# One planned schedule, another queue model: a causal-attention and FFN kernel on one core

## The chip, the core and the metric

The kernel runs on one core of a Trainium2 chip. The time is the device time of one execution in microseconds; before the change it is 1059.81 us, the median of three runs (1059.1 to 1061.09). TensorE (PE) multiplies matrices, VectorE (DVE) and ScalarE (ACT) work element by element and on rows, GpSimd (POOL) does the same for data in on-chip memory, and the queue of SyncE (SP) issues all DMAs. Each engine executes its instructions in the order in which they stand in the program; a semaphore holds an instruction, and all behind it on that engine, until its data is there.

## The reference

```python
q, k, v: (8, 8, 576, 64) float32        # batch, heads, positions, width of a head
scores = q @ k.T / sqrt(64), masked where block_i < block_j   # blocks of 64 positions
attn   = exp(scores - max); attn = attn / (sum + 1e-9)
x      = (attn @ v), heads side by side -> (4608, 512)
h      = x @ w_in                       # (512, 2048)
g      = h * clip(h + 3, 0, 6) / 6
out    = g @ w_out                      # (2048, 512)
```

## The kernel before

The attention of one batch element and two heads is a *slot*; there are 32, numbered n. A slot has three groups g of three blocks of 64 query rows. The FFN works on pieces of up to 384 rows of x, and each piece on 16 blocks f of 128 columns of w_in.

To keep the accuracy of float32, a float32 matrix is split into two float16 parts, high and low, and a product is the sum of three float16 products. Slots 0 to 3 and the first FFN piece, which run while the weights are still being split, are computed in float32 instead (functions with 32 in their name).

A slot n from 4 on goes like this: qk loads q and k, qks splits them, a DMA transpose makes qkT; TensorE makes the scores s; VectorE takes row maxima (st), ACT the exponentials p with their sums, and VectorE and ACT the normalised, split probabilities phl; DMA transposes make pT, one for g = 0 (phl_0), one for g = 1 (phl_1), three for g = 2 (phl_6 to phl_8); TensorE multiplies with vhl into pv: pv_0 for groups 0 and 1, pv_1 for group 2. VectorE and ACT write the result to x. pT01, which holds the transposed probabilities of groups 0 and 1, has one buffer. FFN: h = x, win; ACT and VectorE make r and g; o = g, wout, which is stored by way of osb.

In slots 0 to 3 TensorE transposes itself: scores sf, exponentials pf, transposes pt, result pf by pT. The sums are applied differently there (`pv_group32`, L940): the reciprocals of three row sums become three diagonal blocks rd (a 128x64 identity, each row times its reciprocal); TensorE multiplies rd with a block matrix of ones (pr), so that the reciprocals stand along the free dimension, and ACT copies it to rb. Three rd make one pr, and there are 12 of these groups.

**What sets the order.** No instruction is issued when the program's text reaches it. A `Recorder` takes all of them, finds their dependencies, and `schedule` (L260) plays them through a plan: for each engine a clock, for each instruction a cost from a formula (`cost`, L205), for each buffer a time at which it comes free. Whenever an engine is free in the plan it takes the ready instruction with the lowest key; the keys come from tables of due times (AT for slots, FT for FFN pieces, AS and RT for the float32 slots, and so on, L26 to L55). An instruction that two engines can do (`scaled`, L144) goes to the one that the plan sees finish it earlier. The instructions are emitted in the order of their planned starts. So a change of one cost can move the order on all engines.

A DMA in the plan before: it lands after a fixed time and a time by its size; loads and stores, but not transposes, wait in addition for those before them.

Of the kernel before, what the change touches and what calls it, by code (L numbers as in the profile page):

```python
# [14 lines left out]
ALU = mybir.AluOpType  # L15
# [7 lines left out]
WX = 10  # L23
WY = 27

U = 2.788  # L26
AS = (7.494, 11.408, 15.3, 22.633)
AL = 14.807
PV0 = 2.519
TA, TR, PR = 2.197, 5.661, 0.677  # L30
QR = 3.417
PVA, PVB = 0.93, 1.25
PHS = 18
WLP = 0
WHA = 0
EXA = 8
QTH = False
EVR = 3
EVP = 2
PRO = True  # L40
MEM = 0

NMIN = 64
QL = 0.849
VL = 0.2
W0, WD = 4.938, 2.891
S0, SD = 57.576, 4.59
M0, MD = 34.073, 5
RT = (25.619, 42.369, 59.881, 71.242)
RS, RL, VL1 = 2.796, 15.216, 24.0  # L50
VM0, VMX = 10.452, 0.3
AT = ((4, 86.25), (6, 128.63), (8, 159.32), (10, 199.92), (12, 240.31), (14, 287.79), (16, 335.13), (24, 565.96), (32, 826.62))
FT = ((0, 28), (1, 100), (2, 168.81), (3, 239.13), (4, 279.57), (5, 356.87), (7, 505.16), (10, 740.96), (13, 988.23))
QP = 0.55
VP = 0.5  # L55
BLK = 64
EXPONENT_BITS = 0x7F800000
# [3 lines left out]
class Op:  # L61

    __slots__ = ("ways", "key", "preds", "joint", "n", "start", "end", "tiles", "eng", "half")


class Engine:
# [9 lines left out]
        return call  # L78


ADV = {("tensor", "a"): 60.0}


class Recorder:
# [3 lines left out]

    NAMES = ("tensor", "vector", "scalar", "gpsimd", "sync")
    LAT = {"tensor": 55, "vector": 37, "scalar": 39, "gpsimd": 65, "sync": 65}  # L90
    TURN = 95
    BIAS = {"vector": 250.0, "gpsimd": 500.0}
    EDGE = 0.0
# [66 lines left out]
    def add(self, ways):  # L160
        eng, method, args, kw = ways[0]
        outs, ins = self.operands(args, kw)
        last = self.ops[-1] if self.ops else None
        if eng == "tensor" and self.joint is not None and last and last.joint == self.joint:
            op = last
            calls, occ, _, _ = op.ways[eng]
            more, took, _ = self.cost(eng, method, args, kw, outs, ins)
            op.ways[eng] = (calls + [(method, args, kw)], occ + more, occ + took, False)
        else:
            op = Op()  # L170
            op.joint, op.n, op.ways = None, len(self.ops), {}
            for e, m, a, k in ways:
                op.ways[e] = ([(m, a, k)], *self.cost(e, m, a, k, *self.operands(a, k)))
            op.key = self.key - self.adv.get((eng, self.cls), 0.0)
            op.preds, op.tiles, op.start = {}, [], None
            op.half = eng == "tensor" and outs[0].ap[0][1] <= 64 and method == "matmul"
            if eng == "tensor":
                op.joint = self.joint
            self.ops.append(op)
        for a, w in [(a, False) for a in ins] + [(a, True) for a in outs]:  # L180
            if self.on_chip(a):
                self.touch(op, a, w)

    def touch(self, op, a, w):
# [17 lines left out]
        keep.append((op, w, p0, p1, b0, b1))  # L202
        self.hist[t.name] = keep

    def cost(self, eng, method, args, kw, outs, ins):  # L205


        n = self.count(outs[0])
        if method == "dma_start":
            nb = mybir.dt.size(outs[0].dtype)  # L210
            for _, c in list(outs[0].ap):
                nb *= c
            if kw.get("transpose"):
                occ = max(1290, 172 * nb / 32768 - 150)
                return occ, occ + (1100 if nb <= 4 * 32768 else 2100), False
            if eng == "gpsimd":
                return 1300, 2900 + nb / 170, False
            return 600, 2000 + nb / 170, False
        if eng == "vector":
            if method == "tensor_reduce":  # L220
                n = self.count(ins[0])
            else:
                ptr = any(isinstance(a, bass.AP) and self.count(a) == 1 for a in args[2:] if n > 1)
                ptr = ptr or n == 1 and method == "tensor_scalar_mul" and isinstance(args[2], bass.AP)
            wide = [a for a in ins if self.count(a) > 1 and not self.psum(a)]
            port = len(wide) > 1
            if method in ("tensor_scalar", "tensor_copy") and n > 1:
                if not any(self.psum(a) for a in outs + ins):
                    if len(outs[0].ap) == 2 or outs[0].ap[1][1] % 2 == 0:
                        n = n / (4 if mybir.dt.size(outs[0].dtype) + mybir.dt.size(ins[0].dtype) == 4 else 2)  # L230
                        port = True
            occ = 68 + 1.042 * n
            if method != "tensor_reduce" and ptr:
                occ += 57
            return occ, occ + 80, port
        if eng == "scalar":
            occ = 94 + 0.8335 * n
            if isinstance(kw.get("scale"), bass.AP):
                occ += 95
            if isinstance(kw.get("bias"), bass.AP):  # L240
                occ += 58
            if "accum_out" in kw:
                occ += 93
            return occ, occ + 105, False
        if eng == "gpsimd":
            if method == "memset":
                return 20 + 1.0 * n, 50 + n, False
            occ = 75 + (2.0 if method == "tensor_tensor" else 1.1) * n
            return occ, occ + 30, True
        f32 = mybir.dt.size(ins[0].dtype) == 4  # L250
        occ = max(n / 2.37, 26) * (4 if f32 else 1) + 2
        if f32 and method == "matmul":
            occ = max(occ, 200)
        if method == "transpose":
            occ = max(occ / 2, 100)
        if outs[0].ap[0][1] <= 64 and method == "matmul":
            occ = occ / 2
        return occ, occ + 172, False

    def schedule(self):  # L260
# [17 lines left out]
        for tag in want:  # L278
            if need[tag].max() > bufs[tag]:
                i = int(need[tag].argmax())  # L280
# [20 lines left out]
        dma = 0.0  # L301
        half = False
# [21 lines left out]
        while done < N:  # L324
            e = min((x for x in self.NAMES if pend[x] or avail[x]), key=lambda x: now[x], default=None)
            if e is None:
                raise RuntimeError("no order")
            t = now[e]
            p, a = pend[e], avail[e]
            while p and p[0][0] <= t:  # L330
                r, k = heapq.heappop(p)
# [5 lines left out]
            if e != "tensor":  # L337
                i = 0
                while i < len(a):
# [4 lines left out]
                    r = room(ops[k], t, full)  # L344
                    if r is None:
                        ways = ops[k].ways
                        if len(ways) == 1:
                            r = t
                        else:

                            mine = t + ways[e][2] + self.BIAS.get(e, 0.0)
                            r = min(
                                max(now[q], ready[k][q]) + ways[q][2] + self.BIAS.get(q, 0.0)
                                for q in ways if q != e
                            )
                            r = t if r >= mine else max(t + 50.0, t + mine - r)
# [6 lines left out]
            else:  # L363
# [4 lines left out]
                for i, (key, k, rd) in enumerate(a):  # L368
# [3 lines left out]
                    r = room(ops[k], t, full)  # L372
                    if r is None:
                        first.setdefault(h, i)
                        if h:
                            got_half += 1
                            for x in ops[k].tiles:
                                if x not in got:
                                    rd = max(rd, min(free[self.meta[x][0]]))
# [3 lines left out]
                if first:  # L383
# [6 lines left out]
                    i = first[h]  # L390
# [14 lines left out]
            o = ops[pick]  # L405
            calls, occ, took, shared = o.ways[e]
# [6 lines left out]
            if shared:  # L413
                t = max(t, port["gpsimd" if e == "vector" else "vector"])
                port[e] = t + took - 60.0
            if e == "tensor" and o.half != half:
                half = o.half
# [2 lines left out]
            o.eng, o.start, o.end = e, t, t + took  # L420
            while head < N and ops[head].start is not None:
                head += 1
            if calls[0][0] == "dma_start" and not calls[0][2].get("transpose"):
                nb = (took - (2900.0 if e == "gpsimd" else 2000.0)) * 0.8
                dma = max(dma, o.end - nb - 400.0) + nb
                o.end = max(o.end, dma + 400.0)
            now[e] = t + occ
            self.busy[e] += occ
            for x in o.tiles:
# [5 lines left out]
            for s, flow in succ[pick]:  # L435
                rs = ready[s]
                for q in rs:
                    r = t if q == e and (e == "tensor" or not flow) else o.end + self.LAT[q]
                    rs[q] = max(rs[q], r)
                ndep[s] -= 1  # L440
                if not ndep[s]:
                    for q in rs:
                        heapq.heappush(pend[q], (rs[q], s))
# [12 lines left out]
def kernel(  # L456
# [13 lines left out]
    nc = Recorder(tc.nc)  # L470
# [92 lines left out]
    ident2 = wpool.tile([P, BLK], F32, tag="ident2", name="ident2")  # L563
# [376 lines left out]
    def pv_group32(n, g):  # L940
        t = pT.pop((n, g))

        r = sums.pop((n, g))
        nc.vector.tensor_scalar(r, r, 1e-9, 1.0, op0=ALU.add, op1=ALU.mult)
        nc.vector.reciprocal(r, r)
        rd = sm.tile([P, GB, BLK], F32, tag="rd", bufs=2, name=f"rd{n}_{g}")
        for i in range(GB):
            nc.gpsimd.tensor_scalar(rd[:, i], ident2, r[:, i:i + 1], 1.0, op0=ALU.mult, op1=ALU.mult)
        if g == 0 or PRO:
            o = 2 if g else len(n_ev) % 3  # L950
            pr = ps_o.tile([P, GT], F32, tag=f"o{o}", name=f"pr{n}_{g}")
# [11 lines left out]
        for j in range(nj):  # L963
            i0 = max(0, 2 * j - 3 * g)
            kp = BLK if 2 * j + 1 > 3 * g + 2 else P
            a = i0 * NU[g] + j
            us = slice(a, a + (GB - 1 - i0) * NU[g] + 1, NU[g])
            for h in range(2):
# [4 lines left out]
                    start=(j == 0),  # L973
# [390 lines left out]
    for n in range(NPAIR):  # L1364
        t = AS[n]
        at(t, qk_load32, n, lead=AL)
        at(t, v_load, n, lead=AL)
# [6 lines left out]
    for n in range(NPAIR):  # L1374
        t = RT[n]
# [9 lines left out]
    for n in range(NPAIR, NSLOT):  # L1385
        t, d = line(AT, n), line(AT, n + 1) - line(AT, n)
# [86 lines left out]
```

## Time and profile before

| | us |
|---|---|
| median of 3 runs | 1059.81 (1059.1 to 1061.09) |
| profiled execution, span from first to last instruction | 1063.1 |
| last ACT instruction of that execution (the last osb) begins | 1059.37 |
| TensorE busy | 995.4 |
| VectorE busy | 833.9 |
| ScalarE busy | 635.8 |
| GpSimd busy | 75.9 |
| mean granted clock of TensorE | 0.980 of full |

No time of the profiled execution other than its span is shown; the span is 3.3 us above the median of the runs.

How to read it: a row of instructions names the engine, the operation, the tile written, an arrow and the tiles read, with buffer numbers left out. A line of waits says which engine's instruction waited for which other, for how many us in total, how often, and the longest. Since all instructions are emitted by the recorder, nearly all of them carry the same line (L452), and one goes by the names of tiles.

### The profile page before, as it was taken

The page shows a single profiled execution, that of the slowest core. Times are in us where ns is not written, and L with a number is a line of the kernel's source. Part 1 is how long each engine was busy: PE and PEld are TensorE (multiplying, and loading weights), DVE is VectorE, ACT ScalarE, POOL GpSimd, SP SyncE. Part 2 cuts the span into 40 slices and gives each one's busy share as a digit, 9 for nine tenths or more (in the row PEclk, how much of TensorE's full clock was granted, in tenths as well). Part 3 has the DMA queues.
Part 4 walks back from the last instruction along what each step waited for, and adds up shares of the span by engine and source line. Part 5 has one row for each costly group of instructions (what it writes and reads, how often), then busy time and mean ns, then how long its engine had stood idle before and what let it go on. Part 6 is the DMA issues. An engine that isn't in the chain of part 4 may idle for free. (4 is left out here: it accounts for less than half of the span.)

```text
span 1063.1 us, 28968 instructions
## 1 busy us (share of the span) xinstructions
PE 995.4 (94%) x11588; PEld 726.0 (68%) x11588; DVE 833.9 (78%) x2308; ACT 635.8 (60%) x1548; POOL 75.9 (7%) x259
## 2 busy tenths in 40 slices
PE   6978967999999999999999999999999999999998
PEld 4645646776777867667766666777767777777776
DVE  4888999999999999899899889787898875332322
ACT  4668757666657676666776565566556563343332
POOL 3132220000000000000000000000000000000000
PEclk8998988999999999999999999999999999999999
DMA  6756546898889887888888779647656533000000
GB/s 157 189 166 180 141 111 140 140 185 156 152 159 171 153 152 143 147 164 149 156 143 181 133 116 167 118 77 143 117 90 128 92 80 57 1 31 2 31 1 31
DMA packets 414199, 128.90 MB, mean 121 GB/s; under 512 B 403184, under 2 KB 403440, under 8 KB 414064
## 3 DMA queue, kind: packets, MB, share of 16 engines
q1 hardware_dynamic: 414064, 127.05, 61.4%
q8 instruction: 91, 1.49, 0.6%
q14 instruction: 44, 0.36, 0.1%
HBM read 45.09 MB, written 9.44 MB: 51 GB/s over the span
## 5 line engine op out<-in xcount | busy, mean ns | idle before, releaser
L452 PE MATMUL h<-x,win 128*64 128x384 f16 (+2 forms) x4720 | 437.0, 321 | 1.8 <-DVE win L452 1.6
L452 PE MATMUL o<-wout,g 128*64 128x512 f16 (+3 forms) x3444 | 430.9, 381 | 2.2 <-DVE g L452 2.2
L452 PEld LDWEIGHTS <-win 128*64 128x64 f16 x4608 | 296.8, 110 | 69.9 <-issue 2.2
L452 PEld LDWEIGHTS <-g 128*64 128x64 f16 x3360 | 221.6, 110 | 105.9 <-issue 2.0
L452 ACT ACTIVATE r<-h,eg,sh 128x384 f32<-128x384 f32 (+1 forms) x240 | 137.1, 593 | 131.5 <-PE h L452 130.8
L452 ACT ACTIVATE p<-s,st,esc 128x64 f32<-128x64 f32 (+1 forms) x280 | 163.1, 587 | 73.6 <-DVE st L452 53.6
L452 DVE SCALAR_TENSOR_TENSOR r<-r,eg,h 128x384 f32<-128x384 f32 (+1 forms) x192 | 113.4, 592 | 116.1 <-ACT r L452 116.0
L452 DVE SCALAR_TENSOR_TENSOR phl<-p,st,phl 128x128 f16<-128x128 f32 (+4 forms) x252 | 135.3, 582 | 0.7 <-ACT phl L452 0.6
L452 ACT ACTIVATE g<-r 128x384 f16<-128x384 f32 (+1 forms) x165 | 84.5, 513 | 85.8 <-DVE r L452 84.9
L452 DVE SCALAR_TENSOR_TENSOR g<-r,g 128x384 f16<-128x384 f32 (+1 forms) x192 | 102.7, 535 | 29.9 <-ACT g L452 29.4
L452 DVE TENSOR_REDUCE st<-s 128x1 f32<-128x64 f32 (+1 forms) x280 | 120.0, 447 | 4.1 <-PE s L452 3.8
L452 PE MATMUL s<-qkT 128*64 128x64 f16 (+7 forms) x1120 | 99.0, 289 | 10.0 <-ACT p L452 6.4
L452 PEld LDWEIGHTS <-vhl 128*64 128x64 f16 x1680 | 72.3, 111 | 41.2 <-issue 25.3
L452 PE MATMUL pv<-pT,vhl 128*64 128x192 f16 (+2 forms) x1680 | 75.1, 235 | 24.8 <-DMA pT<-phl 20.8
L452 ACT ACTIVATE phl<-p,st 128x256 f16<-128x256 f32 (+4 forms) x135 | 70.4, 556 | 34.4 <-DVE st L452 18.7
L452 PEld LDWEIGHTS <-qkT 128*64 128x64 f16 x1120 | 60.0, 111 | 35.4 <-issue 13.0
L452 POOL MEMSET p<- 128x64 f32 x140 | 21.4, 154 | 521.4 <-DVE phl L452 492.5
L452 ACT ACTIVATION_READ_ACCUMULATOR p<-s,st,esc 128x1 f32 x280 | 55.1, 197 | 0.0
L452 DVE TENSOR_SCALAR phl<-p,st 128x512 f16<-128x512 f32 (+4 forms) x117 | 46.0, 424 | 1.8
L452 DVE SCALAR_TENSOR_TENSOR qks<-qk,rs_q,qks 128x576 f16<-128x576 f32 x56 | 44.7, 817 | 0.0
L452 ACT ACTIVATE x<-pv 128x192 f16<-128x192 f32 (+1 forms) x61 | 22.0, 360 | 33.4 <-PE pv L452 30.7
L452 DVE TENSOR_REDUCE qkmx<-qk 128x2 f32<-128x1152 f32 x28 | 37.6, 1344 | 1.6 <-DMA qk<-in_k_dram 1.6
(154 smaller groups left out, 819.4 us busy)
## 6 DMA issues: line engine op xcount, KB each, us to landing
out_dram<-osb SPq DMA_DIRECT2D x35, 256.0 KB, 2.5
vnat<-in_v_dram SPq DMA_DIRECT2D x64, 128.0 KB, 2.9
qk<-in_q_dram SPq DMA_DIRECT2D x28, 288.0 KB, 3.6
qk<-in_k_dram SPq DMA_DIRECT2D x28, 288.0 KB, 4.4
rawo<-in_moe_w_out_dram SPq DMA_DIRECT2D x15, 512.0 KB, 4.6
rawi<-in_moe_w_in_dram SPq DMA_DIRECT2D x14, 512.0 KB, 4.0
pT<-phl SPq DMA_TRANSPOSE x140, 3.4
vnat<-in_v_dram SPq DMA_DIRECT2D x32, 32.0 KB, 2.7
```

What stands on the lines that cost most here:

```text
L452: getattr(eng, method)(*args, **kw)
```

## The change

1. In the plan every DMA, transposes included, goes through one queue: it begins at the earliest `lead` after its issue and after the one before it has ended, takes its bytes by a rate, and has landed `tail` after that; three kinds (load, store, turn) with three sets of numbers. An instruction of TensorE that depends on a DMA is planned 1250 ns after that (`MARGIN`).
2. The cost formulas of a DMA transpose and of ACT's sums are changed.
3. rd may be made by ACT or VectorE, and no longer by GpSimd.
4. The tables of due times are refitted. `EVP` decides in which memory bank the transposes pt of slots 0 to 3 land.

```diff
-U = 2.788
+U = 2.847
...
-QL = 0.849
+QL = 1.341
...
-EVP = 2
+EVP = 4
...
-ADV = {("tensor", "a"): 60.0}
+ADV = {("tensor", "a"): 67.44}
...
+    MARGIN = {"tensor": 1250.0}
+    QUEUE = {"load": (4137.0, -1860.0, 256.0), "store": (4137.0, -1860.0, 580.0), "turn": (4074.0, -2300.0, 182.0)}
...
+            op.queue = self.queue(args, kw) if method == "dma_start" else None
...
+    def queue(self, args, kw):
+
+        nb = mybir.dt.size(args[0].dtype)
+        for _, c in list(args[0].ap):
+            nb *= c
+        kind = "turn" if kw.get("transpose") else "load" if self.on_chip(args[0]) else "store"
+        lead, tail, rate = self.QUEUE[kind]
+        return lead, tail, nb / rate
...
-                occ = max(1290, 172 * nb / 32768 - 150)
+                occ = max(1290, 189 * nb / 32768 - 200)
...
             if "accum_out" in kw:
                 occ += 93
+                return occ, occ + 195, False
...
-            if calls[0][0] == "dma_start" and not calls[0][2].get("transpose"):
-                nb = (took - (2900.0 if e == "gpsimd" else 2000.0)) * 0.8
-                dma = max(dma, o.end - nb - 400.0) + nb
-                o.end = max(o.end, dma + 400.0)
+            margin = {}
+            if o.queue:
+                lead, tail, work = o.queue
+                dma = max(t + lead, dma) + work
+                o.end = dma + tail
+                margin = self.MARGIN
...
-                    r = t if q == e and (e == "tensor" or not flow) else o.end + self.LAT[q]
+                    r = t if q == e and (e == "tensor" or not flow) else o.end + self.LAT[q] + margin.get(q, 0.0)
...
         for i in range(GB):
-            nc.gpsimd.tensor_scalar(rd[:, i], ident2, r[:, i:i + 1], 1.0, op0=ALU.mult, op1=ALU.mult)
+            nc.scaled(rd[:, i], ident2, r[:, i:i + 1], "AV")
```

The instructions of TensorE and SP are the same ones in another order. On the other engines some that can be done by two have changed place: VectorE has 2300 instead of 2310, ACT 1244 instead of 1198, GpSimd 228 instead of 264; the rd are 25 on ACT and 11 on VectorE, where 36 were on GpSimd.

What moves is seen in the order of the instructions. The SP queue in slot 21, before and after (pT21 is written from phl21; qkT22 belongs to the next slot, qk24 and vnat are loads for later slots):

```order
L452 DMA_TRANSPOSE pT21_0_1605<-phl21_0_1611 128x8x128
L452 DMA qk24_1736<-in_q_dram 128x9x64
L452 DMA qk24_1736<-in_k_dram 128x9x64
L452 DMA_TRANSPOSE qkT22_1627<-qks22_1621 128x27x128
L452 DMA vnat2_100<-in_v_dram 128x4x64 x2
L452 DMA vnat2_100<-in_v_dram 64x2x64
L452 DMA_TRANSPOSE pT21_0_1605<-phl21_1_1636 128x18x128
```

```order
L467 DMA_TRANSPOSE pT21_0_1606<-phl21_0_1612 128x8x128
L467 DMA qk24_1751<-in_q_dram 128x9x64
L467 DMA qk24_1751<-in_k_dram 128x9x64
L467 DMA_TRANSPOSE pT21_0_1606<-phl21_1_1627 128x18x128
L467 DMA_TRANSPOSE qkT22_1642<-qks22_1636 128x27x128
L467 DMA vnat2_100<-in_v_dram 128x4x64 x2
L467 DMA vnat2_100<-in_v_dram 64x2x64
```

The transpose of phl21_1, on which pv21_0 waits, has moved ahead of the transpose of qks22 and of the loads of v.

TensorE at the last score block of slot 3 (sf3_8_1 is the second half of its scores, pf3_8 their exponentials, pt3_8_0 the transposes of these):

```order
L452 MATMUL sf3_8_1_549<-qkf3_0_180,qkf3_2_182 128x256
L452 MATMUL pt3_8_0_570<-ident_89,pf3_8_550 128x128
L452 MATMUL mb_q5_608<-qkmx5_603,one_96 64x2 x2
L452 MATMUL pt3_8_0_570<-ident_89,pf3_8_550 128x128
L452 MATMUL pt3_6_0_552<-ident_89,pf3_6_511 128x128 x4
```

```order
L467 MATMUL sf3_8_1_549<-qkf3_0_180,qkf3_2_182 128x256
L467 MATMUL o0_1_312<-wout_86,g0_11_493 64x256 x2
L467 MATMUL pr3_1_516<-rd3_1_515,halves_95 128x192
L467 MATMUL o0_0_311<-wout_86,g0_11_493 128x512
L467 MATMUL h0_13_557<-x0_81,win_85 128x192
L467 MATMUL pt3_6_0_552<-ident_89,pf3_6_502 128x128 x3
L467 MATMUL mb_q4_525<-qkmx4_520,one_96 64x2 x2
L467 MATMUL pt3_6_0_552<-ident_89,pf3_6_502 128x128
L467 MATMUL h0_13_557<-x0_81,win_85 128x192 x2
```

The transpose pt3_8_0 stood straight behind its scores; now it follows after these rows and after h0_13, o0_0, o0_1, mb_w5, h1_0 and pt3_7.

The diagonals of slot 0, group 2: on GpSimd before, on ACT now.

```order
L452 TENSOR_SCALAR sgo1_1_201<-rawo1_1_200 128x512
L452 TENSOR_SCALAR rd0_2_334<-ident2_94,sums0_2_242 128x64 x3
L452 MEMSET pf2_6_447 128x64
L452 TENSOR_SCALAR wout_86<-wout_86,rsio_88 128x512
L452 TENSOR_SCALAR rd1_1_378<-ident2_94,sums1_1_308 128x64 x3
```

```order
L467 ACTIVATE abo1_0_293,wacc1_290<-wout_86 128x512
L467 ACTIVATE rd0_2_331<-ident2_94,sums0_2_238 128x64 x3
L467 ACTIVATE pT1_1_344<-pt1_3_0_345 128x256
L467 ACTIVATE exi2_0_222<-x1_82 128x512
L467 ACTIVATE win_85<-win_85,rsio_88 128x2x256
```

They stood among GpSimd's work on the weights; they now stand among ACT's, between the maxima of one weight block (abo) and the copy of transposes of slot 1.

More of the change, by code (lines that the diff above doesn't have):

```diff
@@ L24 @@
 WY = 27
-U = 2.788
[L27 to L32, printed above, removed]
+U = 2.847
+AS = (7.494, 11.408, 15.3, 22.979)
+AL = 20.256
+PV0 = 2.145
+TA, TR, PR = 2.432, 5.661, 0.677
+QR = 3.473
+PVA, PVB = 0.916, 1.038
 PHS = 18
@@ L43 @@
 NMIN = 64
-QL = 0.849
[L45 to L54, printed above, removed]
+QL = 1.341
+VL = 0.415
+W0, WD = 5.472, 2.891
+S0, SD = 57.672, 4.668
+M0, MD = 33.973, 5.111
+RT = (24.007, 40.757, 58.269, 69.63)
+RS, RL, VL1 = 2.796, 28.901, 29.883
+VM0, VMX = 12.417, 0.323
+AT = ((4, 86.25), (6, 128.63), (8, 159.32), (9, 178.32), (10, 199.92), (12, 240.31), (14, 287.79), (16, 335.13), (24, 565.96), (32, 826.62))
+FT = ((0, 28), (1, 100), (2, 168.81), (3, 239.13), (4, 279.57), (5, 362.65), (7, 510.94), (10, 757.38), (13, 994.01))
+QP = 0.221
 VP = 0.5
@@ L61 @@
 class Op:
-    __slots__ = ("ways", "key", "preds", "joint", "n", "start", "end", "tiles", "eng", "half")
+    __slots__ = ("ways", "key", "preds", "joint", "n", "start", "end", "tiles", "eng", "half", "queue")
 class Engine:
```

## The prediction

> **What bounds the kernel now.** I read the page's busy lines first, then the same by stage, then TensorE's waits, and last the rows around the longest waits.
>
> ```profile
> span 1063.1 us, 28968 instructions
> PE 995.4 (94%) x11588; PEld 726.0 (68%) x11588; DVE 833.9 (78%) x2308; ACT 635.8 (60%) x1548; POOL 75.9 (7%) x259
> PEclk8998988999999999999999999999999999999999
> ```
>
> TensorE is busy 995.4 of 1063.1 us, so 67.7 us of idle time is the most that any order of the same work can win back, plus what the lowered clock costs (the digits of 8 at the start). The multiset of TensorE's instructions is the same before and after, so its work is no term. The stages, as windows over the span (columns: window, its length, busy PE, PEld, DVE, ACT, POOL, granted clock, DMA share, GB/s):
>
> ```profile
> 0.00:40.00 40.00, 30.33 (x138) 19.11 (x139) 22.44 (x66) 22.16 (x79) 10.85 (x41) 0.91 0.68 169
> 40.00:100.00 60.00, 50.44 (x282) 33.51 (x282) 50.08 (x130) 43.45 (x111) 18.43 (x25) 0.89 0.60 174
> 100.00:180.00 80.00, 65.13 (x473) 41.50 (x473) 77.73 (x210) 57.76 (x143) 18.00 (x36) 0.91 0.60 140
> 180.00:330.00 150.00, 144.47 (x1899) 110.36 (x1896) 144.94 (x431) 96.73 (x239) 6.85 (x37) 1.00 0.87 153
> 330.00:630.00 300.00, 283.61 (x3853) 207.42 (x3851) 275.77 (x808) 204.27 (x509) 12.90 (x72) 0.99 0.83 152
> 630.00:893.60 263.60, 255.72 (x3166) 188.98 (x3162) 213.77 (x584) 153.66 (x364) 8.84 (x48) 1.00 0.61 111
> 893.60:1063.10 169.50, 165.68 (x1794) 125.11 (x1794) 49.16 (x85) 57.77 (x106) 0.00 (x0) 1.00 0.04 15
> ```
>
> TensorE's idle time is 34.1 us in the first 180 us, 5.5 to 330, 16.4 to 630, 7.9 to 893.6 and 3.8 after it. From 893.6 on there is only FFN work behind an idle rest of the chip; nothing can be won there. VectorE is the second limit: it idles 17.6, 9.9 and 2.3 us in the first three stages and 5.1 and 24.2 in the next two. So between 100 and 330 us a wait of TensorE taken away is worth little unless VectorE's queue gets shorter too. Who TensorE waits for (total us, times, longest), first over the span, then to 180 us, to 630 and to 1063:
>
> ```profile
> PE pv L452 <- DMA pT<-phl: 20.8, 20, 2.5
> ...
> PE pr L452 <- POOL rd L452: 8.3, 5, 2.9
> PE pt L452 <- ACT pf L452: 8.3, 6, 6.1
> PE s L452 <- ACT p L452: 3.3, 1, 3.3
> ...
> PE pv L452 <- DMA pT<-phl: 15.8, 13, 2.5
> ...
> PE pv L452 <- DMA pT<-phl: 5.0, 7, 1.4
> ```
>
> After 180 us it is one thing: the PV matmul stands at the head of TensorE's queue while the transposed probabilities are still in a DMA. The clock is a second cost of the same waits. The windows in which the trace grants half the clock:
>
> ```profile
> 20.97:27.80 6.83, 6.18 (x24) 3.70 (x24) 1.97 (x5) 2.76 (x9) 0.29 (x1) 0.50 0.94 290
> 61.93:65.35 3.42, 3.42 (x13) 2.34 (x12) 2.49 (x6) 2.88 (x9) 0.15 (x1) 0.50 0.13 13
> 79.00:89.24 10.24, 7.43 (x20) 5.06 (x21) 7.66 (x20) 7.19 (x18) 3.48 (x7) 0.50 0.37 107
> 140.44:147.27 6.83, 3.78 (x17) 3.08 (x18) 6.12 (x19) 3.54 (x11) 0.49 (x3) 0.50 0.24 77
> 167.75:174.57 6.82, 3.53 (x42) 3.09 (x43) 6.82 (x24) 5.62 (x13) 1.23 (x2) 0.50 0.71 143
> 437.40:440.81 3.41, 3.41 (x28) 1.82 (x24) 2.57 (x7) 1.52 (x6) 0.30 (x2) 0.50 0.69 130
> 587.59:591.00 3.41, 3.41 (x24) 1.52 (x22) 2.38 (x10) 0.33 (x1) 0.15 (x1) 0.50 0.90 166
> ```
>
> The first three stand at or behind waits for POOL's rd, the fourth at the 6.1 us wait for ACT, the fifth at the 3.3 us wait, the last two behind the longest two waits for pT. TensorE is busy 31.2 us in them; at half the clock at most half of that, 15.6 us, is lost.
>
> **The change part by part.** *Readers of DMAs planned 1250 ns later, all DMAs in one modelled queue.* It adds no instruction. The two longest pT waits in the timeline, the second with the queue that issued the transpose (columns: start, us, engine, line, instruction, idle time before it and its releaser):
>
> ```profile
> 436.91 0.96 PE L452 MATMUL pv<-pT,vhl 128*64 128x192 f16 x16 [2.03 <-DMA pT<-phl]
> ...
> 572.61 5.24 SPq L452 DMA_TRANSPOSE qkT<-qks  x1
> 577.90 0.61 DVE L452 SCALAR_TENSOR_TENSOR phl<-p,st,phl 128x384 f16<-128x384 f32 x1
> 577.96 1.75 SPq L452 DMA_DIRECT2D vnat<-in_v_dram  x3
> 579.88 8.19 SPq L452 DMA_TRANSPOSE pT<-phl  x2
> 583.41 0.84 PE L452 MATMUL o<-wout,g 128*64 128x512 f16 x6
> 586.77 0.85 PE L452 MATMUL pv<-pT,vhl 128*64 128x192 f16 x18 [2.52 <-DMA pT<-phl]
> ```
>
> Before the second, VectorE delivers phl at 578.5, but SP still issues the 27-block qkT transpose (5.24 us) and three loads of v, and starts on pT at 579.88. In the new order of SP this slot has phl21_1 ahead of both. Over the 28 slots, qkT is issued between the first and second transpose of the slot in 24 before and in 8 now. It isn't the whole cause: the slots that had no qkT in between wait too. The mean wait is 20.8/20 = 1.04 us, under the 1.25 us margin, and the longest would keep 2.52 - 1.25 = 1.27. Bounds: 20.8 us gained, or nothing, if VectorE and not the DMA is what is late. I take 60%, 12.5 us, since VectorE has 5.1 + 24.2 us of idle time left between 180 and 630. With no wait near 2 us the last two clock windows go as well: half of 3.41 + 3.41, 3.4 us (bounds 0 and 3.4). Together -15.9.
>
> The Trainium skill, "TensorE: Matmul & The Clock Gate", section on HAM oscillation, has the clock fall only where TensorE idles longer than about 3.4 us. Here windows stand behind waits of 2.0 and 2.5 us, so the trace does not agree on the length; by the page alone the 3.4 us would not be there to win, and this term would be -12.5.
>
> Cost of the margin: pv later by 1.25 us keeps pT01 (one buffer) and phl2 occupied that much longer. Behind pv stand only h and o of the FFN, for which VectorE and ACT have been ready; I price it at nothing. If that cover is gone, each of 28 slots pays up to 1.25 us, 35 us: the upper bound of the unknown.
>
> *rd off GpSimd.* 36 instructions go; 25 land on ACT, 11 on VectorE.
>
> ```profile
> 56.62 3.89 POOL L452 TENSOR_SCALAR rd<-ident,sums 128x64 f32<-128x64 f32 x3 [1.16 <-DVE sums L452]
> ...
> L452 POOL TENSOR_SCALAR rd<-ident,sums x36: 313/320/2799, 10.7 to 147.5; 128x64 f32<-128x64 f32 x36
> L452 POOL TENSOR_SCALAR wout<-wout,rsio 128x512 f16<-128x512 f32 x7 | 7.1, 1013 | 26.9 <-DVE rsio L452 13.8 <-DVE sums L452 11.5 <-DVE wm L452 1.6
> L452 POOL TENSOR_SCALAR sgo<-rawo 128x512 f32<-128x512 f32 x7 | 5.5, 783 | 7.3 <-DVE sums L452 4.2 <-DVE wout L452 1.7 <-ACT abi L452 1.5
> L452 ACT ACTIVATE phl<-p,st 128x128 f16<-128x128 f32 x35 | 12.7, 392 | 7.0 <-DVE st L452 4.2 <-DVE esc L452 2.4 <-issue 0.3
> L452 ACT ACTIVATE pT<-pt 128x128 f32<-128x128 f32 x12 | 3.3, 275 | 2.8 <-PE pt L452 2.8
> L452 DVE TENSOR_SCALAR phl<-p,st 128x128 f16<-128x128 f32 x21 | 5.7, 289 | 0.6
> L452 DVE TENSOR_SCALAR dg_w<-ident,dg_w 2x2 f32<-2x2 f32 x8 | 1.7, 210 | 0.0
> ```
>
> (In the second row: shortest, median and longest in ns; in the others after the bar busy us and mean ns.) Three rd, 313 ns each at best, took 3.89 us on POOL ahead of the 2.9 us wait. On ACT one costs between 275 and 392 ns, I take 0.33: 8.3 us in a stretch (40 to 180) where ACT idles 38.8; hidden, save that an exp queued behind three rd comes 1 us later: +2 by estimate (bounds 0 and 12 groups x 1 = 12). On VectorE between 210 and 289, 0.25: 2.8 us, two thirds of it where VectorE is full: +1.8. What goes is 8.3 us of waits and, in the three windows behind them, half of 6.18 + 3.42 + 7.43, 8.5 us: 16.8 at most, 0 at least. VectorE's idle time in these stages (17.6 + 9.9, the first much of it the start) caps it; I take -6.
>
> The Trainium skill, "SBUF — State Buffer", section "Who interferes with whom", has a GpSimd instruction that reads SBUF and a VectorE one with two SBUF inputs shut each other out for a whole instruction. The 3.89 us agree: VectorE ran such instructions beside it. By that rule VectorE gains too; that result is the first rival.
>
> *Refitted tables.* They reorder everything to 180 us. The 6.13 us wait ahead of pt3_8 came straight behind sf3_8_1 (order above): the exp and its row maximum had no time. Now some fifteen groups of matmuls stand between. But in that wait VectorE did not idle:
>
> ```profile
> 140.00:143.10 3.10, 0.00 (x0) 0.00 (x0) 3.10 (x8) 0.64 (x3) 0.00 (x0) 0.57 0.00 0
> ...
> DVE vmax L452 <- DMA vnat<-in_v_dram: 8.0, 5, 2.4
> ```
>
> So of 6.1 + 3.3 us and half of 3.78 + 3.53 us, 13.1 in all, I take VectorE's idle time in that stage, -2 (bounds 0 and 13.1). VectorE's own waits for loads of v (8.0 us between 180 and 630) shrink with the later v_max; this is in the 60% above. New waits that another order brings: +4, by estimate; bounds 0 and the 35 above.
>
> **Sum.** -15.9 + 2 + 1.8 - 6 - 2 + 4 = -16.1. The profiled execution has a span of 1063.1, which lies 3.3 us over the median of the runs, 1059.81; the step is the same for both: 1063.1 - 16.1 = 1047.0 in a profile, 1043.7 for the median. I say 1044.
>
> **The rivals.** *VectorE freed (larger gain).* If POOL's rd also held VectorE up, for the shortest rd, 36 x 0.313 = 11.3 us, VectorE's queue in 40 to 330 us shortens, and the terms for rd and the tables double or better: -16.1 - 8 - 6 = -30, 1030. For it speaks that rd stands in the stages where VectorE is full; against it that POOL keeps other instructions of 783 to 1013 ns each there.
>
> *VectorE is late anyway (small gain).* 144.94 of 150 us busy: TensorE's waits for pT are then VectorE's lateness in another dress, and move to s, h and o. Left are the gain after 630 us, where VectorE idles 49.8 (5.0), a clock window or two (3.4) and a little at the start: -5 to -7, 1054.
>
> *The margin doesn't do what it says.* It counts from planned times; if the plan runs over 1.25 us ahead of the chip, the pv come no later against their data. Then -6 - 2 + 3.8 and new waits of 4: about 1059.6, no change.
>
> *The waits collect (slower).* TensorE runs further ahead of VectorE, stalls at s, for banks that exp has not read, in fewer and longer waits; each over 2 us brings a window of 3.41 us at half clock, 1.7 us lost. The 16.4 + 5.5 us of idle time stay, and eight such windows (two now) add 6 x 1.7 = 10; with rd's exps 2 late and nothing won at the start but 6: 1059.8 + 10 + 2 - 6 = 1066. It decides from where VectorE idles under some 10 us between 180 and 630 (29.3 now). For it: fullness of VectorE; against: of 20 pT waits only two brought a window.
>
> **How the numbers follow.** The forecast (1036 to 1052) 0.50; larger gain (to 1024) 0.13; small gain (1052 to 1057.5) 0.15; no change 0.06; slower 0.16. About 0.2%, 2.1 us, is what a measurement of this kernel can tell from no change. Faster by more: 0.78; within it: 0.06; slower: 0.16. The range leaves out a tenth at either end: 1029 to 1063.
>
> **What would show it.** The forecast is right if waits of pv for pT fall under 9 us, none of them near 2; if pr waits for nothing over 1 us; if half-clock windows are four or fewer; and if TensorE's idle time to 180 us falls from 34.1 to about 26. The small gain shows as the same idle time between 180 and 330 under other names (s, h, o waiting for DVE or ACT). The slower case shows as new windows at 0.50 after 180 us. The forecast is wrong in size if VectorE's idle time between 40 and 330 us stays at 17.3.

## The result

The changed kernel takes 1027.58 us, the median of four runs (1027.22 to 1028.61); the kernel before takes 1060.45 (1059.1 to 1065.02) beside it. The ratio is 0.968, with an interval of 0.9643 to 0.9717: 33 us less, where the forecast was 16 and its range ended 1.4 us above the measured time. The profiled execution has a span of 1026.8 us and a mean granted clock of 0.988 (0.980 before).

The page of the changed kernel: its span, the busy times, and the granted clock in 40 slices.

```profile
span 1026.8 us, 28995 instructions
PE 989.4 (96%) x11588; PEld 723.3 (70%) x11588; DVE 826.4 (80%) x2298; ACT 650.9 (63%) x1594; POOL 62.1 (6%) x223
PEclk9999989999999999999999999999999999999999
```

TensorE's idle time is 1026.8 - 989.4 = 37.4 us; it was 67.7. So 30.3 of the 36.3 us between the two spans are idle time (the medians lie 32.9 us apart), and 6.0 are shorter work: TensorE is busy 21.4 us in windows at half the clock, where it was 31.2, and half of that difference is 4.9 us. The first five windows of the prediction's table, and two of those at half the clock:

```profile
0.00:40.00 40.00, 31.99 (x165) 20.69 (x166) 25.87 (x84) 24.93 (x88) 6.92 (x29) 1.00 0.70 183
40.00:100.00 60.00, 55.38 (x327) 34.74 (x325) 58.42 (x147) 55.39 (x149) 13.68 (x16) 1.00 0.69 200
100.00:180.00 80.00, 68.45 (x564) 46.07 (x566) 74.67 (x212) 56.60 (x147) 12.64 (x22) 0.87 0.57 122
180.00:330.00 150.00, 146.08 (x1945) 111.18 (x1942) 147.66 (x438) 105.20 (x257) 7.39 (x41) 0.99 0.96 165
330.00:630.00 300.00, 296.43 (x4003) 216.10 (x4001) 287.62 (x843) 212.77 (x524) 13.65 (x75) 1.00 0.87 156
...
100.44:107.27 6.83, 5.91 (x16) 3.12 (x15) 4.86 (x13) 4.62 (x14) 1.89 (x4) 0.50 0.53 155
...
243.80:247.21 3.41, 3.41 (x36) 2.71 (x34) 3.29 (x13) 2.86 (x6) 0.15 (x1) 0.50 1.07 229
```

TensorE idles 8.0, 4.6 and 11.6 us in the first three stages, 24.2 to 180 us (34.1 before), then 3.9 and 3.6 (5.5 and 16.4). VectorE's idle time fell too: 1.6 us in the second stage (9.9 before), 2.3 in the fourth (5.1), 12.4 in the fifth (24.2); in the third it rose, from 2.3 to 5.3. The half-clock windows that remain are five, 23.9 us in all (the first and the last are shown; seven and 41.0 before), and none stands behind a wait for pT.

A window holds other work in each kernel. So here is the same by place in the program: when TensorE ends the last score block of a slot, and how long it has idled until then (the trace, lined up with the order of the instructions).

| to the end of slot | end before, us | end after | idle before, us | idle after | gained in idle time |
|---|---|---|---|---|---|
| 4 | 167.4 | 151.5 | 30.8 | 20.7 | 10.1 |
| 8 | 262.5 | 250.2 | 37.9 | 27.5 | 10.4 |
| 11 | 330.3 | 317.8 | 39.6 | 28.1 | 11.5 |
| 23 | 629.6 | 604.3 | 56.0 | 31.7 | 24.3 |
| last instruction | | | 63.9 | 33.6 | 30.3 |

(The idle time after TensorE's last instruction, 3.8 us in both kernels, is not in this table.) A third is gained by slot 4, nothing much from there to slot 11, and two thirds later.

TensorE's waits, the five largest and those for rd (total us, times, longest):

```profile
PE h L467 <- DVE r L467: 5.1, 3, 3.5
PE qt L467 <- DMA qf<-in_q_dram: 3.0, 2, 2.9
PE o L467 <- DVE g L467: 2.8, 4, 1.3
PE pt L467 <- ACT pf L467: 2.8, 6, 1.1
PE s L467 <- ACT p L467: 2.1, 6, 0.6
...
PE pr L467 <- ACT rd L467: 1.6, 2, 0.8
...
PE pr L467 <- DVE rd L467: 0.7, 1, 0.7
```

The largest row of before, pv waiting for pT, 20.8 us, has no successor: no such wait is left anywhere. pr waits 2.3 us instead of 8.3, pt for pf 2.8 instead of 8.3. All waits together are 31.9 us instead of 61.4: kinds of wait that shrank did so by some 46 us, and kinds that are new or grew add some 17, the largest h for r with 5.1 (pr for rd is counted as one kind, whichever engine makes rd).

The new diagonals (in ns: shortest, median, longest; then the time of the first and last):

```profile
L467 ACT ACTIVATE rd<-ident,sums x25: 331/338/356, 12.2 to 130.5; 128x64 f32<-128x64 f32 x25
L467 DVE TENSOR_SCALAR rd<-ident,sums x11: 236/249/255, 19.5 to 113.5; 128x64 f32<-128x64 f32 x11
```

And the chain that ended last, by engine (before: PE 21%, DVE 0%):

```profile
PE 28%; DVE 7%; DMA 1%; ACT 1%; issue 1%; SPq 0%; ACTq 0%; DVEq 0%
```

These shares can't be compared as they stand, because the chain can be followed further back here: to 625 us, where it ended at 822 us before. From 790 us on VectorE has no share of it in the changed kernel; its 7% lie earlier, where the chain of before doesn't reach.

### The profile page after: what moved, and what is told of

Same layout as the page of the kernel before. It is cut to its first block, busy times and chain, and to the rows that moved or that the text cites. A ratio compares the mean times of both kernels' runs of the same rounds, so it can differ in the third digit from the quotient of the medians.

```text
span 1026.8 us, 28995 instructions
## 1 busy us (share of the span) xinstructions
PE 989.4 (96%) x11588; PEld 723.3 (70%) x11588; DVE 826.4 (80%) x2298; ACT 650.9 (63%) x1594; POOL 62.1 (6%) x223
## 5 line engine op out<-in xcount | busy, mean ns | idle before, releaser
L467 ACT ACTIVATE g<-r 128x384 f16<-128x384 f32 (+1 forms) x161 | 82.1, 510 | 86.5 <-DVE r L467 85.1
L467 DVE SCALAR_TENSOR_TENSOR phl<-p,st,phl 128x256 f16<-128x256 f32 (+4 forms) x252 | 135.6, 582 | 0.6 <-ACT phl L467 0.2
L467 ACT ACTIVATE phl<-p,st 128x128 f16<-128x128 f32 (+4 forms) x147 | 75.1, 547 | 32.3 <-DVE st L467 13.9
L467 PEld LDWEIGHTS <-vhl 128*64 128x64 f16 x1680 | 73.1, 111 | 15.5 <-issue 5.4
L467 DVE TENSOR_SCALAR phl<-p,st 128x384 f16<-128x384 f32 (+4 forms) x105 | 42.8, 434 | 1.4
L467 DVE TENSOR_SCALAR st<-st,esc 128x3 f32<-128x3 f32 (+1 forms) x168 | 34.3, 211 | 0.5
```

Source lines behind the costliest of these rows:

```text
L467: getattr(eng, method)(*args, **kw)
```

## The experiments

Three questions were open. Does planning the readers of DMAs later take waits away, or move them to another name (the price of the margin)? What are rd's 36 instructions worth, and by what way: the waits of pr, or the hold that GpSimd has on VectorE? And what do the tables and the queue's model do? The expectations name their theories themselves. The kernel before took 1060.45 to 1067.02 us on the chips of these runs, so ratios to it are compared; a ratio of 0.01 is some 10.6 us, and the changed kernel stands at 0.968. Two kinds of kernel were made. *In place*: the order is kept and only one kind of instruction is moved or given to another engine. *Planned*: one piece of the plan is put in or taken out, and the whole order follows.

### The margin in place, in the order of before

After planning, every instruction keeps its planned start as its key, and only pv is moved; what depends on it, or takes a buffer it uses, moves along.

```diff
-        for o in self.schedule():
+        order = self.schedule()
+        key, last = {}, {}
+        for o in order:
+            want = o.start
+            if o.tag.startswith("pv"):
+                want = max(want + 1250.0, last.get(o.tag, 0.0) + 0.001)
+            for p in list(o.preds) + o.after:
+                want = max(want, key[p] + 0.001)
+            key[o.n] = want
+            last[o.tag] = want
+        order = sorted(order, key=lambda o: key[o.n])
+        for o in order:
...
```

> The kernel before with its own order, in which only the pv matmuls are moved back by 1.25 us of planned time (other instructions keep their order, save those that must follow a pv). Theory M (TensorE read too early, being 1.25 us later is what counts): pv's waits for pT fall from 20.8 us to under 6, the two half-clock windows after 400 us go, about 1060 - 18 = 1042. Theory V (VectorE is what is late): the waits turn up at s, h and o, the time stays within 4 us of 1060. Theory T (the refitted due times carry the gain, being later alone is not enough): pv's waits fall by half at most, about 1050.

1075.28 us, ratio 1.0104 (1.0057 to 1.0151): slower. TensorE's waits in this kernel:

```profile
PE s L472 <- DVE x L472: 14.9, 23, 1.2
PE s L472 <- ACT p L472: 8.9, 18, 3.3
...
PE pv L472 <- DMA pT<-phl: 5.7, 11, 1.2
```

The waits for pT fell from 20.8 to 5.7 us. But s now waits 14.9 us for VectorE's x, in 23 places, and 8.9 for ACT's p. One of these places in the timeline:

```profile
240.66 0.33 ACT L472 ACTIVATE x<-pv 128x192 f16<-128x192 f32 x1 [3.13 <-PE pv L472]
...
241.03 0.36 DVE L472 SCALAR_TENSOR_TENSOR x<-pv,x 128x192 f16<-128x192 f32 x1 [0.78 <-ACT x L472]
...
241.44 0.62 PE L472 MATMUL s<-qkT 128*64 128x512 f16 x4 [0.81 <-DVE x L472]
```

pv's result is a tile in the same three banks as the scores. It holds its bank until ACT and VectorE have read it into x, and the next score block, one instruction further on, waits for that bank. So the wait is not for data but for a place to write, and it has moved by one instruction. TensorE's idle time to the end is 67.4 us (63.9), only 3.5 more. The other 8 us of the span are longer work: 5.6 of it up to the end of slot 4, with a half-clock window of 13.66 us (25.22 to 38.88 us) before any pv where there was one of 6.83, and 2.5 behind it, although the two half-clock windows after 400 us are gone. Why the work there is longer isn't shown.

The opposite, pv moved 1.25 us forward in the changed order (-1250.0 in the place of 1250.0):

> The changed kernel with its own order, in which only the pv matmuls are moved forward by 1.25 us of planned time. If the margin is what keeps pv from waiting: pv waits 8 to 20 us for pT, about 1027 + 13 = 1040. If the order around pv would do without it: pv waits under 4 us, within 3 us of 1027.

1052.82 us, ratio 0.9864 (0.9804 to 0.9923): more than half of the gain is gone. Its waits of pv:

```profile
PE pv L487 <- ACT p L487: 15.5, 24, 2.9
...
PE pv L487 <- DMA pT<-phl: 4.0, 6, 1.9
```

pv waits again, 19.5 us in these two rows. But only 4.0 of it shows as the DMA; 15.5 us is the bank that ACT's exponentials have to free. Moved in either direction by hand, pv collides with the scores for the banks.

### The margin planned

The changed kernel with the margin taken out of the plan (`MARGIN = {}`), and the kernel before with nothing but the margin put in:

```diff
+    MARGIN = {"tensor": 1250.0}
...
+            margin = self.MARGIN if calls[0][0] == "dma_start" else {}
...
-                    r = t if q == e and (e == "tensor" or not flow) else o.end + self.LAT[q]
+                    r = t if q == e and (e == "tensor" or not flow) else o.end + self.LAT[q] + margin.get(q, 0.0)
```

> The changed kernel planned without the margin (queue model, costs, rd and tables stay). Theory M2 (the margin pays, but only in a plan that moves the rest of TensorE's order with it): pv's waits for pT are back at 12 us or more, about 1045. Theory Q (the one DMA queue in the plan carries the gain): waits under 6 us, about 1030. Theory C (the later sums of ACT carry it): the same, about 1030.

> The code and tables before, planned with the margin alone (readers of DMAs on TensorE 1.25 us later in the plan). Theory M2 (the margin pays where the plan moves the rest with it): the 13 us that the changed kernel loses without the margin, about 1048; pv's waits for pT under 5 us and s waits for DVE under 5 us. If the margin needs the queue model or the tables with it: waits like those of the in-place move, 1060 to 1070.

Without the margin: 1043.09 us, 0.9811 (0.9784 to 0.9839). The margin alone: 1047.5 us, 0.9825 (0.9779 to 0.987). The waits for pT in the one and in the other, and the next rows of the latter:

```profile
PE pv L467 <- DMA pT<-phl: 11.0, 14, 2.5
```

```profile
PE s L454 <- ACT p L454: 7.1, 8, 2.7
...
PE pv L454 <- DMA pT<-phl: 5.3, 7, 1.5
PE s L454 <- DVE x L454: 3.7, 2, 2.1
```

Taking it out costs 0.0131, 13.9 us; putting it in wins 0.0175, 18.5 us. The idle time behind slot 11 shows where: from slot 11 to 23 TensorE idles 3.6 us in the changed kernel, 9.4 without the margin, 16.4 before. Planned, the same 1.25 us that lost 1% in place wins 1.8%: the plan keeps a time for each bank, and s waits for x 3.7 us instead of 14.9. How the order does it isn't shown. Distance alone it is not: a score block stands straight behind pv's last matmul 16 times in the kernel moved by hand, 6 times in this one, and 17 times in the changed kernel, where s never waits for x.

Not all of the 18.5 us is pv's wait, either. In this kernel the waits of the first four slots are shorter too, before there is any pv:

```profile
PE pt L454 <- ACT pf L454: 2.5, 6, 1.0
PE pr L454 <- POOL rd L454: 2.5, 4, 1.6
```

Both were 8.3 us. Of the 17.3 us of idle time that it wins, 4.4 are won by the end of slot 4: the margin changed the order of these slots as well.

Is more better? A longer margin (1900 ns), and a margin for VectorE's readers too (`{"tensor": 1250.0, "vector": 600.0}`):

> The changed kernel planned with a margin of 1.9 us in place of 1.25. Its pv no longer wait for pT, so more margin has nothing to win: 1027 to 1033. If waits of pv for ACT and of s for banks are also lateness of the plan: 1022.

> The changed kernel planned with a margin of 0.6 us for VectorE's readers of DMAs too. VectorE waits some 2 us in all for loads after 180 us, so little is to be won: 1025 to 1031.

1035.11 us, 0.9729 (0.9686 to 0.9772), and 1032.11 us, 0.9696 (0.9656 to 0.9736). Neither is better. The first lies 0.5% above the changed kernel, with intervals that overlap.

### The diagonals

In place, both ways: all 36 rd on ACT in the order of before, and all 36 on GpSimd in the changed order.

```diff
+            if o.tag.startswith("rd"):
...
+                o.eng = "scalar"
...
```

(and `"gpsimd"` in the other)

> The kernel before with its own order, in which the 36 rd are made by ACT at the place in the order where GpSimd made them. The forecast's term for rd (-6 + 2 + 1.8): about 1058. If the waits of pr (8.3 us) and half of the windows behind them (8.5 us) go whole: 1044. Theory V: no change, since VectorE is full there: 1060.

> The changed kernel with its own order, in which the 36 rd are made by GpSimd at the place in the order where ACT or VectorE made them. If rd on GpSimd costs its time on the chip: the 11 us of the kernel planned so, about 1039, with pr waiting 8 us or more for rd. If it costs by what the plan makes of it: within 5 us of 1027, pr waiting under 6 us.

On ACT in the old order: 1060.55 us, 0.9969 (0.9943 to 0.9996), some 3 us. On GpSimd in the new order: 1035.79 us, 0.9743 (0.9704 to 0.9782), some 7 us lost, though the interval touches that of the changed kernel (to 0.9717). The waits of the first kernel:

```profile
PE pt L474 <- ACT pf L474: 7.9, 5, 6.1
PE s L474 <- ACT p L474: 6.1, 5, 3.3
PE pr L474 <- ACT rd L474: 4.6, 6, 1.2
```

pr waits 4.6 instead of 8.3 us, but the 6.1 us before pt3_8 and the 3.3 us before s5 stay as they are: they are written into the order. In the second kernel, the busy times, pr's wait, the stage from 40 to 100 us, and the rd themselves:

```profile
PE 990.1 (96%) x11588; PEld 725.6 (70%) x11588; DVE 824.8 (80%) x2287; ACT 645.7 (62%) x1569; POOL 79.2 (8%) x259
...
PE pr L491 <- POOL rd L491: 6.2, 7, 2.4
...
40.00:100.00 60.00, 54.87 (x327) 34.78 (x326) 56.04 (x146) 51.84 (x134) 20.86 (x25) 1.00 0.69 198
...
L491 POOL TENSOR_SCALAR rd<-ident,sums x36: 308/318/1283, 11.9 to 135.7; 128x64 f32<-128x64 f32 x36
```

pr waits 6.2 us instead of 2.3. VectorE is busy 824.8 us without its 11 rd; with them (11 x 0.249 = 2.7) that would be 827.5, against 826.4. So rd on GpSimd adds 1.1 us to VectorE's busy time in all, against 11.3 us in the rival of the prediction. In the old order it is the same: VectorE's 2308 instructions take 832.9 us with rd on ACT and 833.9 with rd on GpSimd.

Planned, both ways: the changed kernel with rd given to GpSimd again, and the kernel before with `nc.scaled(rd, ..., "AV")`.

> The changed kernel planned with rd on GpSimd. If rd is worth its waits and half of the clock windows behind them (16.8 us): about 1044. If it is worth what it was alone in the order of before (0.3%): about 1031. Theories M2, Q and C all say 1031 to 1036.

> The code and tables before, planned with rd on ACT or VectorE. Theory R (the plan uses the freed time; what an instruction costs in place is the small part): the 11 us that the changed kernel loses with rd planned on GpSimd, about 1050, nearly all of it before 260 us. If rd is worth only what it was in place: 1057 to 1060.

The first: 1041.3 us, 0.9789 (0.9757 to 0.9821), 11.6 us lost. The second: 1061.44 us, 0.996 (0.9938 to 0.9983), 4.2 us won. The first kernel's wait of pr, and its stage from 40 to 100 us:

```profile
PE pr L467 <- POOL rd L467: 10.0, 9, 2.9
...
40.00:100.00 60.00, 50.78 (x292) 32.95 (x293) 50.71 (x134) 43.05 (x111) 18.52 (x22) 0.97 0.62 185
```

Here VectorE idles 9.3 us, as it did before (9.9); it was 1.6 in the changed kernel, and 4.0 there with rd moved to GpSimd in place. At the end of slot 8 this kernel is at 264.8 us, the kernel before at 262.5, the changed one at 250.2; from there on it runs like the changed one. So all that rd is worth is won before some 260 us.

### The tables, the queue, and the sums' end

The refitted tables in the code before, and the tables of before in the changed code:

> The code before (its DMA model, no margin, rd on GpSimd) with the refitted tables. Theory M: pv still waits some 15 to 20 us for pT, and the time is between 1050 and 1060. Theory T: pv's waits under 8 us, about 1038.

> The changed code (one DMA queue in the plan, margin of 1.25 us, rd on ACT or VectorE) with the tables of before. Theory M: pv's waits for pT nearly gone, about 1038. Theory T: qkT still stands between a slot's first two transposes in 23 of 28 slots, pv's waits stay above 10 us, about 1052.

1068.74 us, 1.0029 (0.9997 to 1.0061), and 1033.3 us, 0.9712 (0.9665 to 0.976). By themselves the tables win nothing; the changed code without them has all but 3.4 us of the gain. The waits of the first, then of the second:

```profile
PE pv L452 <- DMA pT<-phl: 15.0, 14, 3.2
PE s L452 <- DMA qkT<-qks: 10.3, 10, 1.7
...
PE pt L452 <- ACT pf L452: 1.3, 3, 0.5
```

```profile
PE pv L467 <- DMA pT<-phl: 1.2, 3, 0.5
```

These two also test what the prediction read out of the SP queue. With the new tables, qkT is issued between the two transposes of a slot in 7 slots of 28, as in the changed kernel, and pv waits 15.0 us for pT all the same, while s now waits 10.3 us for qkT. With the old tables in the new code it is in between in 23 slots, and pv waits 1.2 us. So the place of qkT in the queue is not by itself what made pv wait. The tables alone do take away the 6.1 us wait before pt3_8 (pt waits 1.3 us for pf in all, at most 0.5 at once), as the prediction had it; the time doesn't fall with it.

The changed kernel with the old model of a DMA's landing but with the margin, and without the later end of ACT's sums:

```diff
-            margin = {}
-            if o.queue:
-                lead, tail, work = o.queue
-                dma = max(t + lead, dma) + work
-                o.end = dma + tail
-                margin = self.MARGIN
+            margin = self.MARGIN if o.queue else {}
+            if calls[0][0] == "dma_start" and not calls[0][2].get("transpose"):
+                nb = (took - (2900.0 if e == "gpsimd" else 2000.0)) * 0.8
+                dma = max(dma, o.end - nb - 400.0) + nb
+                o.end = max(o.end, dma + 400.0)
```

```diff
             if "accum_out" in kw:
                 occ += 93
-                return occ, occ + 195, False
```

> The changed kernel planned with the DMA model of before, in which transposes don't queue (the margin for readers of DMAs stays). Theory Q: pv and s wait for pT and qkT some 15 us, about 1047. Theory M2: within 5 us of the changed kernel, about 1031. Theory C: the same, about 1030.

> The changed kernel planned with the old end of ACT's instructions with a sum (90 ns earlier). Theory C: s and pv wait for ACT and the readers of p are late, about 1045. Theories M2 and Q: within 4 us of the changed kernel, about 1030.

1032.97 us, 0.971 (0.9687 to 0.9734), and 1030.95 us, 0.9691 (0.9668 to 0.9713). Both intervals hold the changed kernel's 0.968 or come near it. Taken out of the changed kernel, a queue fitted to the trace, the first thing that the change is named for, is worth some 3 us, and the sums' end 1; neither is clear of noise.

Last, the kernel before with two and with three pieces: margin and planned rd, and these with the sums' end.

> Both, with the code and tables before. If the two are the change and add up: 1060 - 12 - 11 = 1037. If the queue model and the costs are needed too: above 1045.

> The code and tables before, planned with the margin, rd on ACT or VectorE, and the later end of ACT's sums. If that cost is what margin and rd lack: pt's wait for pf (10.3 us) and s's for p (7.6) fall to a third, the ratio from 0.980 to about 0.971. If the DMA queue in the plan is: no change, 0.980.

1043.07 us, 0.9802 (0.9732 to 0.9872), and 1040.83 us, 0.9783 (0.9746 to 0.9819). The wait of pt in the one and in the other:

```profile
PE pt L454 <- ACT pf L454: 10.3, 7, 5.0
```

```profile
PE pt L455 <- ACT pf L455: 2.3, 5, 1.0
```

With the later end of the sums 8.0 us of waits at pt are gone; pt needs the exponentials whose end that number plans. But the whole order is planned anew, and the wait comes and goes with other pieces too: with the margin alone pt waits 2.5 us for pf, and 2.0 in the changed kernel without the later end. And the ratio falls only by 0.002, within the noise; h waits 5.3 us for r in two places there, a row that the one without it does not have at that size (1.0).

## Why the prediction was right, and where it was not

**The step that failed: the cap by VectorE's idle time.** The sum was -15.9 for the margin, -2.2 for rd (-6, +2 and +1.8), -2 for the tables and +4 for new waits. Taken out of the changed kernel one at a time, with the new waits in each number, the margin is worth 13.9 us, rd 11.6 and the tables 3.4; the queue's model and the sums' end, which had no term of their own, 3.2 and 1.2. So the margin's term was near, rd's was too small by 9.4 us, and nothing is left of the +4. rd's term came down from a possible 16.8 to 6 by "VectorE's idle time in these stages (17.6 + 9.9, the first much of it the start) caps it; I take -6". Put into the kernel before by itself, rd wins 4.2 us: what it is worth depends on the rest of the plan, and for that the sum had no term.

**What bounds the kernel: right.** Of 67.7 us of idle time 30.3 went, and 6.0 us of busy time, most of it by the clock.

**The margin: right in kind, and its total by luck.** The waits were sized too small, in "I take 60%, 12.5 us, since VectorE has 5.1 + 24.2 us of idle time left": all 20.8 us went. Taking the margin out costs 13.9 us and putting it in alone wins 18.5, so the whole term of -15.9 lies between the two by luck of its parts: the other waits that come with the new order were booked elsewhere.

**"I price it at nothing": wrong in its reason.** "Behind pv stand only h and o" overlooked s and the bank that pv holds. In place, that price is real, 14.9 us at s. It is not paid because the order is planned anew around the later pv; that the plan keeps a time for each buffer could be read in the code. The slower rival named this mechanism, waits collecting at s, and its 1066 us, a ratio of 1.006, is at the lower end of what b_pv_late measured (1.0057 to 1.0151); it didn't reckon with a plan that moves the rest along.

**qkT between the transposes: a misreading.** The prediction counted 24 slots before and 8 now; in the changed kernel it is 7. More than the slip counts that it read a cause from an order: one kernel shows the wait with little of the interleaving, another the interleaving with hardly a wait.

**rd: durations right, worth too small.** 0.33 and 0.25 us were forecast, 0.338 and 0.249 measured. Net -2.2 was forecast; in the changed plan rd is worth 11.6 us, of which some 7 without any new order, and in the old plan 4.2. VectorE's idle time was no cap. Between 40 and 100 us its longest waits before were these:

```profile
DVE dg_w L452 <- PE mt_w L452: 3.8, 2, 2.4
DVE sgi L452 <- ACT abo L452: 1.8, 1, 1.8
DVE rb L452 <- ACT rb L452: 1.7, 1, 1.7
```

It waited for TensorE and ACT, and rb stands straight behind the pr that waited for rd. Afterwards VectorE did 58.42 us of work in these 60 us instead of 50.08, and TensorE 55.38 instead of 50.44. With rd on GpSimd in the changed order VectorE idles 4.0 us instead of 1.6 in this stage, with the order planned anew 9.3. So the smaller part of its idle time goes with rd's engine itself, the larger with the order that the plan makes then. The exponentials that come late behind rd on ACT, priced at +2, can't be told: with rd on ACT in the order of before pt waits 7.9 us for pf (8.3), and with rd planned beside the margin 10.3 instead of 2.5, but in another order.

**Tables: -2 forecast, 3.4 measured where they are taken out** (the intervals overlap), **and nothing where they are put in alone** (1.0029). The prediction read rightly that they take the 6.1 us wait before pt3_8 away. But the margin alone does that as well, and with the tables alone s waits 10.3 us for qkT instead. The sums' end, which the prediction did not price, brings by itself 1 to 2 us.

**New waits, +4 and +3.8 of rd: too small too.** Kinds of wait that are new or grew add some 17 us. So the forecast let 23.9 us of waits and clock go and 7.8 come; measured were 46 of waits and 6.0 of shorter work that went, and 17 that came. Both sides were about half of what came, and so was the difference. What the terms for the margin, rd and the tables share is that VectorE's idle time bounded them. From 180 to 330 us VectorE, busy 144.94 of 150 us before, did more afterwards, 147.66 us.

**The rivals.** *VectorE freed* gave the nearest time, 1030, but by luck, not by its mechanism: rd on GpSimd adds 1.1 us to VectorE's busy time, not 11.3. The Trainium skill, "SBUF — State Buffer", section "Who interferes with whom", has a GpSimd instruction that reads SBUF and a VectorE one with two SBUF inputs shut each other out; the rd on GpSimd agree on their side (308 ns at best, 1283 at worst in the kernel above, 2799 before), while on VectorE's side the busy time shows 1 us. *VectorE late anyway* falls with the idle time between slots 11 and 23, which did not come back under other names (16.4 to 3.6 us). *The margin does nothing* falls with a_margin0.

**What would show it.** Waits for pT under 9 us: none. No wait of pr over 1 us: the longest is 0.8, 2.3 in all. Four windows at half clock or fewer: five. Idle time to 180 us from 34.1 to about 26: 24.2. VectorE's idle time between 40 and 330 us was to fall from 17.3, if the size was right: it fell to 9.2, and the size was wrong all the same, on the other side.

**What stays open.** Taken out one at a time, the five pieces above add up to 33.3 us, close to the 33.9 of the whole. Put into the kernel before, margin and rd bring 18.5 and 4.2, but 21.0 together, 23.0 with the sums; the step from there (0.9783) to the changed code with old tables (0.9712) is 7.5 us, which holds the queue's model and the refitted cost of a transpose, and whose intervals overlap. How much of it is either, or chance of another order, no run tells.

## What to carry to other kernels

An engine's idle time in the profile of before is not a bound on what it lets others win, unless one has followed what it is idle for: here VectorE waited for TensorE and ACT, and with another order much of its idle time went together with theirs. When an instruction is moved behind a late transfer, ask what its result holds until it is read, and who needs that place next; the same move lost 1% by hand and won 1.8% when the planner could move the rest as well. And an order in a queue is not a cause until one kernel has the order without the wait.

## What the runs showed of the hardware

Half the clock comes after shorter waits than the prediction had read from the kernel before, where the shortest that it named ahead of a window was 2.0 us. The window from 100.44 us stands among three short waits of TensorE in the changed kernel:

```profile
98.71 0.59 PE L467 MATMUL pr<-rd,halves 128*128 128x192 f32 x2 [0.84 <-ACT rd L467]
...
100.15 0.88 PE L467 MATMUL pt<-ident,pf 128*128 128x128 f32 x4 [0.85 <-ACT rb L467]
...
103.01 1.22 PE L467 MATMUL o<-wout,g 128*128 128x512 f32 x1 [0.92 <-DVE g L467]
```

Two of 0.84 and 0.85 us lie ahead of it within 2.6 us, and one of 0.92 within it. The Trainium skill, "TensorE: Matmul & The Clock Gate", section on HAM oscillation, asks for over about 3.4 us of idle time; that does not agree with these rows. The sum of the idle time tells more than the longest wait. The half-clock windows last 3.41 us or a multiple of it. In the 3.41 us ahead of each of the twelve windows of the two kernels TensorE idles between 1.60 and 3.41 us in all (1.69 ahead of this one). Divide the rest of each span into stretches of 3.41 us at the same spacing: of those at full clock that full clock follows, leaving out the first at the start, none idles more than 1.50 us but one with 1.95 (before, from 512.5 us). So in these two kernels half the clock followed 1.60 us of idle time or more in such a stretch, and full clock 1.50 or less; the stretch of 1.95 shows that this isn't the whole rule.
